# Sums of h made in place in the last product, and all logits and weight sums in the stage before it

## The chip, the cores and the metric

One core of a Trainium2 chip runs the whole program. Its engines work in parallel, each through its own queue in order: TensorE (PE) multiplies, VectorE (DVE) and ScalarE (ACT) do elementwise work, GpSimd (POOL) and SyncE (SP) issue transfers here. The metric is the device time of one execution in microseconds.

## The reference

With x of 2048 by 640, two DFT matrices per side and a gated feed-forward layer of width 1728, all float32:

```python
def _A_ref(x, dft_seq_re, dft_seq_im, dft_hid_re, dft_hid_im):
    a = jnp.einsum("bsd,ed->bse", x, dft_hid_re)
    b = jnp.einsum("bsd,ed->bse", x, dft_hid_im)
    return jnp.einsum("ts,bse->bte", dft_seq_re, a) - jnp.einsum("ts,bse->bte", dft_seq_im, b)

def _B_ref(x, w_gate, w_up, w_down):
    return (_gelu(x @ w_gate) * (x @ w_up)) @ w_down

g = _sigmoid((x * gate_w).sum(-1, keepdims=True))
return g * _A_ref(...) + (1 - g) * _B_ref(...)
```

## The kernel before, in words

**Arithmetic.** Every float32 operand is split into a high and a low part: ScalarE rounds the block (`high`, L80), VectorE subtracts that from the block (`low`, L83). A product of two blocks is three matmuls, high by high, high by low and low by high (L99 to L101). The large products use one level of a Strassen scheme: seven block products in place of eight, for which sums of blocks are needed on both sides. Such a scheme is run in two passes. A first pass takes the products that need the blocks themselves and one sum, a second pass those that need the other sums; partial results of the first are kept for the second. `X`, `Z`, `V`, `L`, `Q`, `R`, `Y` are the PSUM banks of the products, eight in all, so at a switch from one pass to the next a bank must be copied out (`copy`, L146, on ScalarE, or an addition on VectorE) before its successor starts.

**Stages.** (1) Up to about 325 us: gate and up product with the gelu. The result h is written to device memory in blocks `hA[tp][k]`: half `tp` of the rows, pair `k` of the width's tiles (six pairs), four parts of 128x512 each, b11, b12, b21, b22. (2) The *C stage*, to about 751 us: the sequence DFT times x. 64 steps `i`, each with one 1 MB piece of the matrix (`cra`, `crb`, loaded by `load_c` three steps ahead, split by `split_c` two steps ahead into `ch` and `cl`; in a second pass its sums are `csa` and `csb`). Steps 0 to 7 are a first pass, 8 to 15 a second, and so on in four groups. (3) The *last product* of the feed-forward layer, h by `w_down`, to about 927 us: 28 steps, for each half a first pass of seven and a second of seven (`load_k` three ahead, `split_k` two ahead, `step_k`). Its sums of h for the second pass are T1 = b12 - b11, T3 = b22 - b12, T2 = b22 - T1 and T4 = b21 - T2. (4) The hidden DFT, to the end, which adds onto the output.

**What stands between the steps of the C stage.** Four kinds of small work, each a few loads by SyncE, a few VectorE operations and stores by GpSimd:
- `sum_h` (twelve times, table `HT_AT`): loads the four parts of one `hA` block (`ht`), makes T1 to T4, stores them as `hT`, which the last product's second passes load.
- `sum_wd` (six times, `WD_AT`): sums of `w_down` for both passes (`dr`, `da`), stored as `wsd`.
- `sum_wu` (five times; three here, two in the last product): sums of the hidden DFT's weights (`ur`, `ua`), stored as `wsu`, with negated blocks `wneg`.
- `load_z` (sixteen times; ten here, six in the last product): a tile of x (`xz`), multiplied by `gate_w` and summed to logits in `z`. `gates` makes the sigmoid of the eight logits of one half and stores it and its complement.

`sum_h0_narrow` (twice, in the last product, `lg`) makes sums of the narrow remaining block of h, stored in `hL`.

**What sets the order.** ScalarE and VectorE keep the written order (`in_order`), SyncE's loads of the C stage too; TensorE's is made by a scheduler. Work that is loaded at step i is done at step i+1, after that step's split, so a load that is late holds everything written behind it on VectorE. In the last step of a first pass (7, 23, 39, 55) the split of the step two ahead is held until the first bank's products have been issued (`held`). All large tiles share 46 buffers of 4 KB per partition (`slot`), the 128x512 ones 15 buffers of 2 KB (`mtile`); a load or split waits until an earlier user of its buffer is done, for a stored tile until the store has landed.

Of the kernel before, what the change touches and what calls it, by code (L numbers as in the profile page):

```python
# [9 lines left out]
F32 = mybir.dt.float32  # L10
# [4 lines left out]
P = 128  # L15
# [10 lines left out]
GM_AT = [2,19]  # L26
EORD = [0, 2, 1, 3, 4]
PAIRED = 3
ZB_AT = [5,7,9,14,15,16]
XB_AT = [0, 1, 2, 3, 4, 5, 6, 7]  # L30
WU_AT, WU_DOWN = [18, 34, 49], [10, 17]
HL_AT = [1, 12]


@with_exitstack
def kernel(
# [33 lines left out]
    def slot(dt, shape, name):  # L70
        return pool.tile(shape, dt, tag="s4", name=name, bufs=46)
# [49 lines left out]
    gwb = pool.tile([P, D], F32, tag="gwb", name="gwb")  # L121


    hA, hT = ([[dram.tile([P, 4, T], F32, tag=f"h{n}{p}{k}", name=f"h{n}{p}{k}") for k in range(NK)] for p in range(2)] for n in "AT")
# [75 lines left out]
    def wsmall(dt, name):  # L200
        return pool.tile([P, 2, P], dt, tag="w", name=name, bufs=6)
# [405 lines left out]

    def sum_wd(k):

        r, a21 = slot(F32, [P, 8, P], f"dr{k}"), wsmall(F32, f"da{k}")  # L610
        nc.sync.dma_start(r, wd[k, :, :8])
        nc.sync.dma_start(a21, wd[k, :, 8:])
        return [do for _, do in sums_left(nc.gpsimd, r[:, 0:2], r[:, 2:4], r[:, 6:8], a21, wsd[k])]

    def sum_h(tp, k):


        b11, b12, b21, b22 = (mtile(F32, f"ht{tp}{k}{q}") for q in range(4))
        for q, v in enumerate((b11, b12, b21, b22)):
            nc.sync.dma_start(v, hA[tp][k][:, q])  # L620

        def do():
            tt(b11, b12, b11, op=ALU.subtract)  # L623
            keep(hT[tp][k], 0, b11)
            tt(b12, b22, b12, op=ALU.subtract)
            keep(hT[tp][k], 2, b12)
            tt(b22, b22, b11, op=ALU.subtract)
            keep(hT[tp][k], 1, b22)
            tt(b21, b21, b22, op=ALU.subtract)
            keep(hT[tp][k], 3, b21)  # L630

        return [do]

    def sum_h0(tp):

# [169 lines left out]
    def load_k(i):  # L805


        tp, b, k = kseq[i]
        n = f"{tp}{b}{k}"
        r = None  # L810
        if not (k == NK and b):
            r = slot(F32, [P, 8, P], f"kw{n}")
        if k == NK and b:
            src = hL[tp]
        elif k == NK:
            m = slot(F32, [P, 8, P], f"km{n}")
            d = slot(F32, [P, 8, P], f"kd{n}")
            nc.sync.dma_start(r[:, :5], wd0)
            for q in range(2):
                rows = slice(q * FR, (q + 1) * FR)  # L820
                nc.sync.dma_start(m[rows, :5], wdr)
                nc.sync.dma_start(d[rows, :4], wd0[:FR, :4])
            r, src = (r, m, d), h0[tp]
        elif b:
            nc.sync.dma_start(r[:, 0:2], wd[k, :, 6:8])
            nc.sync.dma_start(r[:, 2:8], wsd[k][:, 0:6])
            src = hT[tp][k]
        else:
            nc.sync.dma_start(r[:, 0:6], wd[k, :, 0:6])
            nc.sync.dma_start(r[:, 6:8], wsd[k][:, 6:8])  # L830
            src = hA[tp][k]
        raw = []
        for q in range(2):
            raw.append(pair(F32, f"kr{n}{q}"))
            nc.sync.dma_start(raw[q], src[:, 2 * q : 2 * q + 2])
        kraw[i] = r, raw

    def split_k(i):
        tp, b, k = kseq[i]
        n = f"{tp}{b}{k}"  # L840
        r, raw = kraw.pop(i)
        B = []

        def right():
            B = []
            for q in range(2):
                v = hl(f"kb{n}{q}")
                split(*v, raw[q])
                B += [at(v, 0), at(v, 1)]
            return B  # L850

        if k == NK and b:
            W = ktile.pop(("left", tp))
# [519 lines left out]
    for i, (j, ri, b, sp) in enumerate(cseq):  # L1373
# [2 lines left out]
        if i + AHEAD + 1 < len(cseq):  # L1376
            load_c(i + AHEAD + 1)
        ready, units = units, []
        if i in HT_AT:
            units += sum_h(*HT_AT[i])  # L1380
        if i in WD_AT:
            units += sum_wd(WD_AT[i])
        if i in ZC_AT:
            (_, first), (_, total) = load_z(1)
            first()
            units.append(total)
# [118 lines left out]
                after.append(tsums)  # L1505
    loads.close()

    zwork, narrow = [], []
    gates(0)
    for i in range(len(kseq)):  # L1510
        if i + 3 < len(kseq):
            load_k(i + 3)
# [16 lines left out]
        if i in GM_AT:  # L1529
            gm[GM_AT.index(i)] = gate_tile(gmd, GM_AT.index(i), f"gm{i}")  # L1530
        step_k(i)
        for do in narrow:
            do()
        narrow = sum_h0_narrow(HL_AT.index(i)) if i in HL_AT else []
        for p, at_i in enumerate(WU_DOWN, len(WU_AT)):
            if i == at_i:
                wus[p] = sum_wu(p)
            if at_i <= i < at_i + 3:
                next(wus[p], None)
        for _, do in zwork[:1]:  # L1540
            do()
        zwork = load_z(1) if i in ZB_AT else []
        for _, do in zwork[:1]:
            do()
        del zwork[:1]
        if i == ZB_AT[-1] + 1:
            gates(1)


    bk = {}  # L1550
# [225 lines left out]
```

## Time and profile before

| | |
|---|---|
| median of 3 runs | 1052.19 us (1050.69 to 1054.45) |
| profiled execution, its own time | 1054.85 us |
| its span, first to last instruction | 1053.1 us |
| TensorE busy | 1024.7 us (97%) |
| VectorE busy | 824.7 us (78%) |
| ScalarE busy | 486.3 us (46%) |
| GpSimd busy | 184.8 us (18%) |
| mean granted TensorE clock | 0.987 |
| moved by DMA | 280.95 MB, mean 267 GB/s |

A row of the timeline reads: start, duration, engine, line, operation, what is written and from what, count, and in brackets how long the engine stood idle before it and what ended that. Consecutive VectorE operations overlap a little, so the distance from one start to the next is what an operation costs the queue. Rows of waits give the total, how many, and the longest. Busy TensorE is not TensorE at its peak; the count of matmuls in a stretch tells more.

### The profile page before, as it was taken

What the parts mean: (1) busy time and instruction counts of PE and PEld (TensorE: products, weight loads), DVE (VectorE), ACT (ScalarE), POOL (GpSimd) and SP (SyncE); (2) the same over time, 40 slices, a digit from 0 to 9 for tenths busy, and PEclk for the clock granted to TensorE, in tenths of its full rate; (3) what the DMA queues carried; (4) which work ended last, traced back from release to release, by engine and by line L of the source; (5) the groups of instructions that cost most, each with busy time, mean ns of one, the idle gap of its engine ahead of it and who ended that gap; (6) DMA issues with size and microseconds to landing.
All of it is one profiled execution on the core that took longest, in us unless ns stands there. A gap on an engine that the chain in (4) does not pass through costs nothing.

```text
span 1053.1 us, 13358 instructions
## 1 busy us (share of the span) xinstructions
PE 1024.7 (97%) x4489; PEld 841.8 (80%) x4489; DVE 824.7 (78%) x1159; ACT 486.3 (46%) x624; POOL 184.8 (18%) x326
## 2 busy tenths in 40 slices
PE   9999999999999999996999899979999899999998
PEld 7888888888888878885888788868887688888887
DVE  8977755474758889856997798779979797996796
ACT  6644545444435744332342334333727736654350
POOL 0221111111201100221123302330210111011112
PEclk9999999999999999998999999989999999999999
DMA  8465455454668966898699889999899998987856
GB/s 308 147 211 196 126 178 162 152 170 137 185 204 292 259 195 215 285 368 281 235 324 378 335 314 312 380 412 384 293 336 374 399 385 325 352 324 219 265 158 98
DMA packets 101188, 280.95 MB, mean 267 GB/s; under 512 B 13504, under 2 KB 24640, under 8 KB 101120
## 3 DMA queue, kind: packets, MB, share of 16 engines
q1 hardware_dynamic: 73536, 194.15, 52.9%
q0 software_dynamic: 27296, 85.76, 25.2%
q8 instruction: 35, 0.57, 0.2%
q14 instruction: 33, 0.27, 0.1%
q10 hardware_dynamic: 288, 0.20, 0.1%
HBM read 205.06 MB, written 70.27 MB: 261 GB/s over the span
## 4 chain that ended last, share of the span: by engine, by line
issue 27%; PE 25%; DMA 7%; POOL 5%; DVE 2%; ACT 1%; SPq 0%; POOLq 0%; DVEq 0%; ACTq 0%
DMA xz<-in_xz 2%; POOL hT L415 1%; POOL uA L1359 1%; POOL uT L1359 1%; DMA ua<-in_wu 1%; DMA crb<-in_ct 1%; DMA ht<-hA 1%; DMA wneg<-ur 1%; PE yX L101 1%; PE yX L99 1%; PE yX L100 1%; PE kX L99 1%; DMA wsd<-dr 1%; PE kX L101 1%; PE kX L100 1%
## 5 line engine op out<-in xcount | busy, mean ns | idle before, releaser
L80 ACT ACTIVATE ch<-csa 128x1024 fp32r<-128x1024 f32 x32 | 34.0, 1062 | 121.0 <-DVE csa L786 107.8
L80 ACT ACTIVATE ch<-cra 128x1024 fp32r<-128x1024 f32 x32 | 33.9, 1058 | 70.1 <-DMA cra<-in_ct 17.1
L415 POOL DMA_DIRECT2D hA<-s x48 | 26.3, 547 | 179.2 <-DVE s L582 160.1
L83 DVE TENSOR_TENSOR cl<-crb,ch 128x1024 fp32r<-128x1024 f32 x32 | 39.1, 1221 | 22.4 <-DMA wsd<-dr 7.9
L415 POOL DMA_DIRECT2D hT<-ht x48 | 26.1, 544 | 157.5 <-DVE ht L623 149.4
L83 DVE TENSOR_TENSOR cl<-cra,ch 128x1024 fp32r<-128x1024 f32 x32 | 39.1, 1222 | 17.5 <-ACT ch L80 9.8
L100 PE MATMUL pL<-cl,xah 128*128 128x512 f32 x128 | 49.8, 389 | 0.0
L101 PE MATMUL pL<-ch,xal 128*128 128x512 f32 x128 | 49.8, 389 | 0.0
L99 PE MATMUL pL<-ch,xah 128*128 128x512 f32 x128 | 49.0, 389 | 0.0
L571 DVE TENSOR_TENSOR s<-s,pX 128x512 f32<-128x512 f32 x24 | 16.4, 685 | 38.5 <-PE pX L101 38.5
L80 ACT ACTIVATE ch<-crb 128x1024 fp32r<-128x1024 f32 x32 | 33.8, 1056 | 25.4 <-PE pL L101 8.9
L83 DVE TENSOR_TENSOR cl<-csb,ch 128x1024 fp32r<-128x1024 f32 x32 | 39.2, 1225 | 4.8 <-ACT ch L80 3.8
L83 DVE TENSOR_TENSOR cl<-csa,ch 128x1024 fp32r<-128x1024 f32 x32 | 39.0, 1220 | 4.6 <-ACT ch L80 3.5
L80 ACT ACTIVATE ch<-csb 128x1024 fp32r<-128x1024 f32 x32 | 33.9, 1060 | 12.0 <-DVE csb L789 6.1
L557 ACT ACTIVATE s<-pZ 128x512 f32<-128x512 f32 x24 | 14.2, 598 | 52.1 <-PE pZ L101 35.3
L99 PE MATMUL pX<-ch,xbh 128*128 128x512 f32 x64 | 25.4, 405 | 12.3 <-ACT ch L80 11.8
L576 ACT ACTIVATE s<-s 128x512 f32<-128x512 f32 x24 | 15.1, 634 | 46.6 <-DVE s L575 46.6
L80 ACT ACTIVATE kh<-kw 128x1024 fp32r<-128x1024 f32 x24 | 25.5, 1064 | 21.8 <-DMA kw<-wsd 21.8
L83 DVE TENSOR_TENSOR kl<-kw,kh 128x1024 fp32r<-128x1024 f32 x24 | 29.3, 1219 | 7.3 <-ACT kh L80 7.3
L146 ACT ACTIVATE s<-pX 128x512 f32<-128x512 f32 x41 | 23.7, 592 | 19.0 <-PE pX L101 18.7
L99 PE MATMUL pQ<-ch,xbh 128*128 128x512 f32 x64 | 26.6, 415 | 5.6 <-ACT s L146 5.6
L101 PEld LDWEIGHTS pL<-ch,xal 128*128 128x128 f32 x128 | 24.0, 188 | 5.0
(3658 smaller groups left out, 3478.5 us busy)
## 6 DMA issues: line engine op xcount, KB each, us to landing
cra<-in_ct SPq DMA_DIRECT2D x64, 512.0 KB, 6.3
crb<-in_ct SPq DMA_DIRECT2D x64, 512.0 KB, 6.4
hA<-s POOLq DMA_DIRECT2D x48, 256.0 KB, 2.9
ht<-hA SPq DMA_DIRECT2D x48, 256.0 KB, 7.8
hT<-ht POOLq DMA_DIRECT2D x48, 256.0 KB, 6.3
kr<-hA SPq DMA_DIRECT2D x24, 512.0 KB, 8.0
kr<-hT SPq DMA_DIRECT2D x24, 512.0 KB, 7.9
ux<-uA SPq DMA_DIRECT2D x24, 512.0 KB, 6.9
```

The costliest lines, as they stand in the source:

```text
L80: nc.scalar.activation(hi, raw, AF.Copy)
L83: nc.vector.tensor_tensor(lo, raw, hi.bitcast(F32), op=ALU.subtract)
L99: nc.tensor.matmul(ps, lh, rh, start=first, stop=False, skip_group_check=True)
L100: nc.tensor.matmul(ps, lh, rl, start=False, stop=False, skip_group_check=True)
L101: nc.tensor.matmul(ps, ll, rh, start=False, stop=last, skip_group_check=True)
L146: nc.scalar.activation(m, src, AF.Copy)
L415: nc.gpsimd.dma_start(to[:, i], src)
L557: nc.scalar.activation(s5, Z, AF.Copy)
L571: tt(s5, s5, X, op=ALU.add)
L576: nc.scalar.activation(s2, s2, AF.Gelu_apprx_tanh)
L1359: nc.gpsimd.dma_start(to[:, i], src)
```

## The change

`sum_h`, `HT_AT` and the blocks `hT` are gone. The second passes of the last product load the blocks `hA` themselves, and `split_k` makes the four sums in place on the loaded tiles before it splits them; since the sums then lie in another order than the products want them, the list that `right` returns is reordered. `sum_wd` loads into two `m` tiles instead of a large one and a small one. All five `sum_wu`, all sixteen logits and both `sum_h0_narrow` stand in the C stage, by tables of step numbers; both `gates` stand at the start of the last product. Two of the splits of x for second passes move from steps 6 and 7 to 9 and 11 (`XB_AT`).

```diff
-ZB_AT = [5,7,9,14,15,16]
-XB_AT = [0, 1, 2, 3, 4, 5, 6, 7]
-WU_AT, WU_DOWN = [18, 34, 49], [10, 17]
-HL_AT = [1, 12]
+XB_AT = [0, 1, 2, 3, 4, 5, 9, 11]
+WU_AT = [17, 19, 33, 35, 50]
+HL_AT = [21, 54]
+Z_AT = [18, 21, 26, 29, 30, 34, 37, 42, 45, 46, 49, 52, 55, 58, 61, 62]
...
     def sum_wd(k):
-        r, a21 = slot(F32, [P, 8, P], f"dr{k}"), wsmall(F32, f"da{k}")
-        nc.sync.dma_start(r, wd[k, :, :8])
-        nc.sync.dma_start(a21, wd[k, :, 8:])
-        return [do for _, do in sums_left(nc.gpsimd, r[:, 0:2], r[:, 2:4], r[:, 6:8], a21, wsd[k])]
-
-    def sum_h(tp, k):
...
+        r = [mtile(F32, f"dr{k}{q}").rearrange("p (b c) -> p b c", c=P) for q in range(2)]
+        nc.sync.dma_start(r[0], wd[k, :, 0:4])
+        nc.sync.dma_start(r[1], wd[k, :, 6:10])
+        return [do for _, do in sums_left(nc.gpsimd, r[0][:, 0:2], r[0][:, 2:4], r[1][:, 0:2], r[1][:, 2:4], wsd[k])]
...
-            src = hT[tp][k]
+            src = hA[tp][k]
...
         r, raw = kraw.pop(i)
+        sums = b and k < NK
+        if sums:
+            (b11, b12), (b21, b22) = ([v[:, q] for q in range(2)] for v in raw)
+            tt(b11, b12, b11, op=ALU.subtract)
+            tt(b12, b22, b12, op=ALU.subtract)
+            tt(b22, b22, b11, op=ALU.subtract)
+            tt(b21, b21, b22, op=ALU.subtract)
...
-            return B
+            return [B[q] for q in (0, 3, 1, 2)] if sums else B
...
-    HT_AT, WD_AT, ZC_AT = {}, {}, [16, 22, 26, 32, 38, 42, 48, 54, 58, 60]
-    for g in range(3):
-        for q, r in enumerate((2, 4, 8, 13)):
-            HT_AT[16 * g + 16 + r] = q % 2, 2 * g + q // 2
-        for q in range(2):
-            WD_AT[16 * g + 19 + 2 * q] = 2 * g + q
+    WD_AT = [20, 22, 36, 38, 51, 53]
...
-        if i in HT_AT:
-            units += sum_h(*HT_AT[i])
         if i in WD_AT:
-            units += sum_wd(WD_AT[i])
-        if i in ZC_AT:
+            units += sum_wd(WD_AT.index(i))
+        if i in HL_AT:
+            units += sum_h0_narrow(HL_AT.index(i))
+        if i in Z_AT:
...
-    zwork, narrow = [], []
-    gates(0)
+    for tp in range(2):
+        gates(tp)
...
-        for do in narrow:
-            do()
-        narrow = sum_h0_narrow(HL_AT.index(i)) if i in HL_AT else []
-        for p, at_i in enumerate(WU_DOWN, len(WU_AT)):
...
-        zwork = load_z(1) if i in ZB_AT else []
...
-        if i == ZB_AT[-1] + 1:
-            gates(1)
```

How it moves instructions, first on VectorE at the switch of the C stage into step 24: from the last operation of the split of step 24 (`cl24_1`) to the first of the split of step 25 (`csa25`). `dr`/`da` are a weight sum, `xz` a logit, `lg` a narrow sum of h. Before:

```order
L83 TENSOR_TENSOR cl24_1_4087<-csb24_4079,ch24_1_4086 128x1024
L597 TENSOR_TENSOR dr1_4020<-da1_4021,dr1_4020 128x256
L598 TENSOR_TENSOR da1_4021<-dr1_4020,da1_4021 128x256
L601 TENSOR_TENSOR dr1_4020<-dr1_4020 128x256
L730 ISA xz1_4074,z_63<-xz1_4074,gwb_64 128x640
L785 TENSOR_TENSOR csa25_4143<-cra25_4070 128x512
```

The change:

```order
L83 TENSOR_TENSOR cl24_1_4067<-csb24_4059,ch24_1_4066 128x1024
L645 TENSOR_TENSOR lg01_3991<-lg01_3991,lg00_3990 128x512
L646 TENSOR_TENSOR lg02_3992<-lg02_3992,lg03_3993 128x512
L648 TENSOR_TENSOR lg02_3992<-lg02_3992,lg01_3991 128x512
L711 ISA xz1_4000,z_63<-xz1_4000,gwb_64 128x640
L597 TENSOR_TENSOR dr11_4053<-dr11_4053 128x256
L598 TENSOR_TENSOR dr11_4053<-dr10_4052,dr11_4053 128x256
L601 TENSOR_TENSOR dr10_4052<-dr11_4053,dr10_4052 128x256
L766 TENSOR_TENSOR csa25_4127<-cra25_4048 128x512
```

Three operations of a narrow sum have come to a logit and a weight sum (of the weight sum one repeated row is left out, L602). At the switch into step 40 a logit and a weight sum stand there, at step 56 a weight sum and a narrow sum, at step 8 nothing.

The same place in SyncE's queue, from the loads of step 24 (`cra24`) to those of step 25. Before:

```order
L777 DMA cra24_4016<-in_ct 128x1024
L777 DMA crb24_4017<-in_ct 128x1024
L611 DMA dr1_4020<-in_wd 128x1024
L612 DMA da1_4021<-in_wd 128x256
L777 DMA cra25_4070<-in_ct 128x1024
```

The change:

```order
L758 DMA cra24_3986<-in_ct 128x1024
L758 DMA crb24_3987<-in_ct 128x1024
L640 DMA lg00_3990<-h00_77 64x512 x2
L640 DMA lg01_3991<-h00_77 64x512 x2
L642 DMA lg02_3992<-h00_77 128x512
L642 DMA lg03_3993<-h00_77 128x512
L707 DMA xz1_4000<-in_xz 128x640
L758 DMA cra25_4048<-in_ct 128x1024
```

Six loads of the narrow sum and one of a logit now stand ahead of the loads of step 25; the weight sum's loads have moved behind them.

Last, VectorE in a second pass of the last product: the split of its step for pair 2 of the first half (`kl` weights, `kb` h), with what stands next to it. Before:

```order
L83 TENSOR_TENSOR kl012_6820<-kw012_6753,kh012_6819 128x1024
L83 TENSOR_TENSOR kb0120l_6824<-kr0120_6756,kb0120h_6823 128x1024
L83 TENSOR_TENSOR kb0121l_6828<-kr0121_6758,kb0121h_6827 128x1024
L730 ISA xz11_6810,z_63<-xz11_6810,gwb_64 128x640
L83 TENSOR_TENSOR kl013_6862<-kw013_6812,kh013_6861 128x1024
```

The change:

```order
L826 TENSOR_TENSOR kr0120_6628<-kr0120_6628 128x512
L827 TENSOR_TENSOR kr0120_6628<-kr0121_6630,kr0120_6628 128x512
L828 TENSOR_TENSOR kr0121_6630<-kr0121_6630,kr0120_6628 128x512
L829 TENSOR_TENSOR kr0121_6630<-kr0121_6630 128x512
L83 TENSOR_TENSOR kl012_6698<-kw012_6625,kh012_6697 128x1024
L83 TENSOR_TENSOR kb0120l_6702<-kr0120_6628,kb0120h_6701 128x1024
L83 TENSOR_TENSOR kb0121l_6706<-kr0121_6630,kb0121h_6705 128x1024
L826 TENSOR_TENSOR kr0130_6689<-kr0130_6689 128x512
```

Four sums stand ahead of each of the ten such splits between the two evacuations (five in each half), and once more per half ahead of the first evacuation; the logits are gone.

More of the change, by code (lines that the diff above doesn't have):

```diff
@@ L121 @@
     gwb = pool.tile([P, D], F32, tag="gwb", name="gwb")
-    hA, hT = ([[dram.tile([P, 4, T], F32, tag=f"h{n}{p}{k}", name=f"h{n}{p}{k}") for k in range(NK)] for p in range(2)] for n in "AT")
+    hA = [[dram.tile([P, 4, T], F32, tag=f"hA{p}{k}", name=f"hA{p}{k}") for k in range(NK)] for p in range(2)]
     h0 = [dram.tile([P, 4, T], F32, tag=f"h0{p}", name=f"h0{p}") for p in range(2)]
@@ L608, in sum_wd @@
     def sum_wd(k):
-        r, a21 = slot(F32, [P, 8, P], f"dr{k}"), wsmall(F32, f"da{k}")
-        nc.sync.dma_start(r, wd[k, :, :8])
-        nc.sync.dma_start(a21, wd[k, :, 8:])
-        return [do for _, do in sums_left(nc.gpsimd, r[:, 0:2], r[:, 2:4], r[:, 6:8], a21, wsd[k])]
-    def sum_h(tp, k):
[L618 to L632, printed above, removed]
+        r = [mtile(F32, f"dr{k}{q}").rearrange("p (b c) -> p b c", c=P) for q in range(2)]
+        nc.sync.dma_start(r[0], wd[k, :, 0:4])
+        nc.sync.dma_start(r[1], wd[k, :, 6:10])
+        return [do for _, do in sums_left(nc.gpsimd, r[0][:, 0:2], r[0][:, 2:4], r[1][:, 0:2], r[1][:, 2:4], wsd[k])]
     def sum_h0(tp):
@@ L1531 @@
         step_k(i)
-        for do in narrow:
-            do()
-        narrow = sum_h0_narrow(HL_AT.index(i)) if i in HL_AT else []
-        for p, at_i in enumerate(WU_DOWN, len(WU_AT)):
[L1536 to L1541, printed above, removed]
-        zwork = load_z(1) if i in ZB_AT else []
-        for _, do in zwork[:1]:
-            do()
-        del zwork[:1]
-        if i == ZB_AT[-1] + 1:
-            gates(1)
     bk = {}
```

## The prediction

> **What bounds the kernel now.** I read the slices first, then the busy time by stretches, then TensorE's waits, then the neighbourhood of each wait on VectorE and in SyncE's queue.
>
> ```profile
> PEclk9999999999999999998999999989999999999999
> DMA  8465455454668966898699889999899998987856
> 400.00:480.00 80.00, 80.00 (x355) 66.24 (x353) 58.39 (x75) 28.38 (x29) 14.11 (x26) 1.00 0.83 297
> 380.00:400.00 20.00, 18.77 (x82) 14.88 (x82) 18.52 (x24) 11.07 (x14) 2.23 (x4) 1.00 0.61 211
> 480.00:520.00 40.00, 30.67 (x123) 24.27 (x122) 33.98 (x48) 13.43 (x16) 8.71 (x16) 0.87 0.73 248
> 580.00:620.00 40.00, 37.24 (x157) 30.30 (x156) 33.54 (x47) 14.07 (x18) 10.32 (x19) 0.96 0.91 333
> 700.00:720.00 20.00, 14.38 (x55) 11.39 (x54) 17.99 (x25) 8.31 (x10) 3.63 (x7) 0.83 1.03 403
> 820.00:860.00 40.00, 35.60 (x146) 28.91 (x145) 34.61 (x45) 24.81 (x29) 7.07 (x13) 0.91 1.03 385
> ```
>
> The stretch rows give, after its length, TensorE's busy time with its matmul count, then weight loads, VectorE, ScalarE, GpSimd, the granted clock, the DMA share and GB/s. At full rate 355 matmuls take 80 us, 0.225 us each. Counts below that rate are TensorE's lost time: in 380:400 6.75 matmuls are missing (88.75 less 82), 1.5 us; in 480:520 54.5, 12.3 us; in 580:620 20.5, 4.6 us; in 700:720 33.75, 7.6 us; in 820:860 31.5, 7.1 us. The first four, **26.0 us**, are the four switches of the C stage from a first to a second pass (steps 8, 24, 40, 56); the last, **7.1 us**, is the switch between the two halves of the last product. The rest runs at TensorE's rate: what this change can win is about 33 us.
>
> ```profile
> PE pX L99 <- ACT ch L80: 11.8, 3, 8.5
> PE pQ L99 <- ACT s L146: 5.6, 1, 5.6
> 601.28 0.50 PE L99 MATMUL pX<-ch,xbh 128*128 128x512 f32 x1 [2.76 <-ACT ch L80]
> 479.13 1.23 DVE L83 TENSOR_TENSOR cl<-crb,ch 128x1024 fp32r<-128x1024 f32 x1 [7.94 <-DMA wsd<-dr]
> SPq L777 <- DMA wsd<-dr: 14.3, 2, 7.8
> 701.79 0.83 DVE L730 CUSTOM_DVE_ANT_0 xz<-xz,gwb 128x640 f32<-128x640 f32 x1 [2.10 <-DMA xz<-in_xz]
> ```
>
> TensorE waits there for a split (`ch`) or for a bank copied behind a split, so VectorE or ScalarE is late. Why it is late differs. At step 24 VectorE stood 7.94 us for a buffer that the store of a weight sum (`dr`) still held. At step 40 SyncE's queue stood 14.3 us in two waits for such buffers and the next blocks were loaded late. At step 56 a logit tile (`xz`) came late while the DMA share was 1.03. At step 40, 2.76 us of idle cost 4.6 us in all: the clock stayed low for the other 1.8.
>
> **The change, part by part. Transfers.**
>
> ```profile
> ht<-hA SPq DMA_DIRECT2D x48, 256.0 KB, 7.8
> 480.27 0.69 DVE L623 TENSOR_TENSOR ht<-ht,ht 128x512 f32<-128x512 f32 x1
> 483.05 0.69 DVE L785 TENSOR_TENSOR csa<-cra 128x512 f32<-128x512 f32 x1
> ```
>
> 48 loads of 256 KB and as many stores go, 25 MB, with twelve blocks of four VectorE operations, 2.78 us each (480.27 to 483.05). The same four operations return in each of the twelve second-pass steps of the last product. Weight sums now stand in the 15 buffers of `m`, so the two waits on `wsd<-dr` above have no such buffer left to wait for; four T buffers per block are no longer asked of `m`, which pays for it.
>
> **The switches.** What came between the last two splits decides. The undisturbed model is step 8, where nothing but two x operations came between.
>
> ```profile
> 381.35 1.23 DVE L83 TENSOR_TENSOR cl<-csb,ch 128x1024 fp32r<-128x1024 f32 x1
> 384.52 0.69 DVE L785 TENSOR_TENSOR csa<-cra 128x512 f32<-128x512 f32 x1
> 386.85 0.39 PE L99 MATMUL pX<-ch,xbh 128*128 128x512 f32 x1
> 702.54 0.69 DVE L785 TENSOR_TENSOR csa<-cra 128x512 f32<-128x512 f32 x1
> 706.78 0.79 PE L99 MATMUL pQ<-ch,xbh 128*128 128x512 f32 x1 [5.62 <-ACT s L146]
> 487.93 0.42 DVE L597 TENSOR_TENSOR dr<-da,dr 128x256 f32<-128x256 f32 x1
> 489.65 0.82 DVE L730 CUSTOM_DVE_ANT_0 xz<-xz,gwb 128x640 f32<-128x640 f32 x1
> 490.39 0.69 DVE L785 TENSOR_TENSOR csa<-cra 128x512 f32<-128x512 f32 x1
> 775.64 0.68 DVE L664 TENSOR_TENSOR lg<-lg,lg 128x512 f32<-128x512 f32 x1
> 777.57 1.22 DVE L83 TENSOR_TENSOR kl<-kw,kh 128x1024 fp32r<-128x1024 f32 x1
> ```
>
> The split of the switch's own step ended at 382.58, 4.27 us before TensorE began that step (386.85); its first six matmuls cover 1.35 more. From the next split's first operation to TensorE going on takes 4.24 us (702.54 to 706.78). So TensorE waits for as long as VectorE works between the two splits, less 1.4 us. A weight sum takes 1.72 us there (487.93 to 489.65), a logit 0.74 (to 490.39), a narrow h sum 1.93 (775.64 to 777.57). After the change the order has, between those splits, at step 8 nothing (two x splits moved to steps 9 and 11): no wait; at step 24 a narrow sum, a logit and a weight sum, 4.39, a wait of 3.0; at step 40 a logit and a weight sum, 2.46, a wait of 1.1; at step 56 a weight sum and a narrow sum, 3.65, a wait of 2.25. To these I add the slow clock: 1.8 for the 3.0 (nearest row: 2.76 idle cost 1.8), half of that for 2.25, none for 1.1; and 2 us in all for loads that still land late, since of the traffic near the switches only part goes. That is 11.05 us of the 26.0 left, **15.0 saved**. Bounds: all 26.0 saved, if splits are made earlier with fewer buffers taken; only 5 saved, if each of the three late switches loses 2.5 to 4 us more to late loads (six loads of the narrow sum stand in SyncE's queue ahead of the next blocks at step 21, and right behind them at 54).
>
> The TensorE page of the Trainium skill (TensorE: Matmul & The Clock Gate, "What you observe" to "What's actually happening") says that the clock halves after an idle window of about 3.4 us. By that alone none of these idles would cost clock, nor would the one of 3.1 us below, and the sum would be 4.5 us lower. The row at 601.28 disagrees: 2.76 us of idle stood in a stretch with a mean clock of 0.96. I keep the row.
>
> **The last product.** TensorE's second-pass step is 24 matmuls, 5.4 us.
>
> ```profile
> 785.21 0.43 DVE L856 TENSOR_TENSOR km<-km 128x256 f32<-128x256 f32 x1 [4.15 <-DMA km<-in_wdr]
> 800.46 1.28 DVE L973 TENSOR_TENSOR ks<-ks,kV 128x512 f32<-128x512 f32 x2
> 802.40 1.22 DVE L83 TENSOR_TENSOR kl<-kw,kh 128x1024 fp32r<-128x1024 f32 x1
> 805.81 1.28 DVE L926 TENSOR_TENSOR ks<-ks,gm 128x512 f32<-128x512 f32 x2
> 808.22 1.22 DVE L83 TENSOR_TENSOR kl<-kw,kh 128x1024 fp32r<-128x1024 f32 x1
> 840.24 1.29 DVE L985 TENSOR_TENSOR ks<-ks,ks 128x512 f32<-128x512 f32 x2
> 842.18 0.80 PE L99 MATMUL kZ<-kb1001h,kh 128*128 128x512 f32 x1 [4.40 <-DVE ksa L985]
> 888.30 1.38 DVE L973 TENSOR_TENSOR ks<-ks,kV 128x512 f32<-128x512 f32 x2 [4.99 <-ACT ks L146]
> 911.34 1.22 DVE L83 TENSOR_TENSOR uw00l<-uw00r,uw00h 128x1024 fp32r<-128x1024 f32 x1
> 918.16 1.22 DVE L83 TENSOR_TENSOR ub11l<-ux,ub11h 128x1024 fp32r<-128x1024 f32 x1
> 927.15 0.39 PE L99 MATMUL yX<-ub00h,uw00h 128*128 128x512 f32 x1
> ```
>
> A split is 3.41 us (802.40 to 805.81); with the sums ahead of it, 6.19, which is 0.8 more than TensorE's step: VectorE now sets the pace there. Between evacuating the first pass (L973) and the second (L985) it has five such splits, 30.95, and four gated outputs, 2.41 (805.81 to 808.22).
>
> First half: before, L973 stood at 800.46. The six loads and the three operations of the narrow sum and the T block ahead of it are gone, and with them most of the 4.15 wait at 785.21; its own split brings 2.78. I take 799 (bounds: 797.6, when TensorE ends that pass, and 803.2). Then 1.2, 30.95, 2.41 and two plain splits, 6.82, reach L985 at 840.4; before it was 840.24, with three logits, a weight sum and load waits in that stretch, all gone now. `kZ`, two operations later (1.94, as 840.24 to 842.18), starts when it did. But TensorE's wait of 4.40 falls apart: 2.7 of it are now spent waiting for splits, so the slow clock, 7.1 less 4.4, **2.7, is saved**. Bounds: 4 saved, 4.3 lost.
>
> Second half: L973 waits for TensorE as before and ends at 889.68. To it come 30.95, 2.41 and the seven plain splits of the next product, 7.96 (911.34 to 918.16 and 1.14): L985 at 931.0. TensorE's last step starts at 923.0 (889.68 and 33.36), ends at 928.4; six matmuls of `yX` reach 929.8; the next product's second banks are free at 932.95. Before, they were taken six matmuls after 927.15, at 928.5. So **4.45 are lost**, with 3.1 of idle and 1.8 of clock, **6.25**. Bounds: 3 (no clock, one step's lateness absorbed) and 9.
>
> What I cost at nothing: both gate steps at the start (VectorE and ScalarE under 0.25 us each, beside the first steps' products); six logits, two narrow sums, two weight sums elsewhere in the C stage, 0.74, 1.93 and 1.72 us of VectorE, hidden while first-pass steps leave it two thirds idle (a first-pass split is 2.4 us against 6.76 of TensorE); if that cover went, they would cost their own length at the next switch, at most 3 us.
>
> **Sum.** 15.0 and 2.7 saved, 6.25 lost: 11.4 less than the profiled execution's 1054.85 (span 1053.1), 1043.4. The median of the runs shown is 2.66 lower, 1052.19: **1041**. By the Trainium skill's rule alone it would be an estimated 1036.
>
> **Rivals.**
> *The switches vanish* (24 in 100). For it: the two waits on `wsd<-dr` are removed at their cause, and 25 MB less lets loads land early. Against it: 2.5 to 4.4 us of sums still stand between the splits. 26.0 and 2.7 saved, 6.25 lost: 1030.
> *The switches stay late* (17 in 100): the DMA share is still near 1 ahead of them, since the narrow sums and a second weight sum took the T blocks' place, and a load that is late holds VectorE in order. Only 8 saved there; 4.5 in all: 1048.
> *VectorE's queue in the second passes costs more than the C stage gives* (11 in 100, slower). In its favour: it has no slack there at all, and its first operation on a block now waits for the load itself. If L973 of the first half comes at 803.2 and one wait like that at 785.21 (4.15) falls into each pass, the halves lose 4.3 and 4.15, then 4.45, 4.15 and 2.7 of clock: 19.8 against 15.0, 1057. It decides once the second passes cost over 18.2. Against it: in the second half the loads were ahead of VectorE from 889 to 919.
> *The forecast* has 48 in 100, and its own range is 1034 to 1048. **Range** for all: 1027 to 1052, from just below the first rival to half way into the last.
>
> A measurement of this kernel tells about 0.3%, 3.2 us, from no change. Faster by more: 47 of the forecast's 48, the 24, and 11 of the 17: 0.82. Within it: 1, 5, and 1 of the slower case: 0.07. Slower, 1 of the 17 and 10 of the last: 0.11.
>
> **What would show it.** No `ht` and no `wsd<-dr` among the waits; the counts of the four switch stretches up from 82, 123, 157 and 55; step 8 without a gap, step 24 still with the longest. In the last product, VectorE without idle between L973 and L985, TensorE waiting for `kb` splits by under 1 us a step, and a new wait of `yZ` for L985 of about 3 us, which was not there. Wrong would be: a wait of the same length at steps 40 and 56 (then late loads, not buffers, made it), `yZ` without a wait (VectorE had slack I did not see), or new waits for `m` buffers in SyncE's queue.

## The result and the profile after

The changed kernel takes 1036.15 us, the median of four runs (1035.35 to 1037.92). The kernel before, run beside it, takes 1053.32. The ratio is 0.984, with a 95% interval from 0.982 to 0.987: 17 us faster, of which the prediction had named 11.

Slices of the changed kernel, for the two rows shown of before:

```profile
PEclk9999999999999999999999999999999999989999
DMA  8556364554567976699769877999899879967856
```

Stretches of the changed kernel (columns as in the prediction). Its times are earlier than before's by whatever was saved up to that point, so step 56 now lies in 680:720, the switch between the halves in 800:840, the end of the last product in 880:920:

```profile
380.00:400.00 20.00, 20.00 (x90) 16.57 (x89) 17.70 (x23) 10.78 (x14) 2.23 (x4) 1.00 0.65 217
480.00:520.00 40.00, 38.99 (x172) 31.89 (x171) 38.61 (x54) 16.95 (x19) 4.90 (x9) 1.00 0.76 253
520.00:540.00 20.00, 18.37 (x81) 14.71 (x81) 14.67 (x21) 8.60 (x11) 2.78 (x6) 1.00 0.62 226
580.00:620.00 40.00, 40.00 (x177) 32.82 (x176) 37.18 (x51) 17.62 (x20) 4.34 (x8) 1.00 0.75 254
680.00:720.00 40.00, 40.00 (x178) 33.15 (x177) 39.52 (x52) 21.21 (x24) 2.72 (x5) 1.00 0.99 353
800.00:840.00 40.00, 37.01 (x158) 30.20 (x157) 39.86 (x48) 23.45 (x27) 3.25 (x6) 0.96 0.82 266
880.00:920.00 40.00, 36.14 (x147) 29.01 (x146) 39.76 (x48) 26.24 (x28) 3.26 (x6) 0.91 0.82 285
```

A full stretch of 40 us holds 177.5 matmuls. The four switches, which had lost 26.0 us, now show 90 in 20 us (step 8; 88.75 is the full rate), 172 (step 24), 177 (step 40) and 178 (step 56). Step 56 runs at TensorE's rate although the DMA share there is still 0.99: traffic alone was not what made it late. A place that lost nothing before now loses 2 us: 520:540, where a second pass gives way to a first (step 32). VectorE is busy for 39.86 and 39.76 of 40 us in the two last stretches, the two ends of the last product's halves.

TensorE's waits in the changed kernel (engine, line, released by: total, times, longest):

```profile
PE yZ L99 <- DVE ksa L973: 3.2, 1, 3.2
PE kZ L99 <- DVE ksa L973: 3.0, 1, 3.0
PE pX L99 <- ACT s L146: 1.6, 1, 1.6
PE pX L99 <- ACT ch L80: 1.0, 1, 1.0
```

Two waits for VectorE's second evacuation (L973, before L985) are the bulk: the known one of `kZ` between the halves, and a new one of `yZ` in the next product. The other two are steps 32 and 24.

The first matmul of the last product shows what the C stage gave back; before, and then the changed kernel:

```profile
751.08 0.39 PE L99 MATMUL kX<-kb0000h,kh 128*128 128x512 f32 x1
```

```profile
728.95 0.39 PE L99 MATMUL kX<-kb0000h,kh 128*128 128x512 f32 x1
```

Read so, from the first matmul of one stage to the first of the next (the last stage to the start of its last matmul), the stages of the profiled executions are these. Most of these executions lie within 1.6 us of the median beside them; that of `no_t` is 3.1 us above it and that of `lead` 3.2 us below. The three parts of the change are: T sums in place, weight sums in `m`, and all logits and sums moved into the C stage.

| kernel | parts | median us | C stage | last product | hidden DFT |
|---|---|---|---|---|---|
| before | none | 1053.3 | 425.8 | 176.1 | 122.4 |
| after | all | 1036.15 | 403.3 | 172.8 | 128.7 |
| `wd_m` | weight sums in m | 1041.4 | 415.9 | 173.1 | 122.4 |
| `t_only` | T in place | 1052.3 | 409.5 | 184.4 | 127.7 |
| `t_wd` | T in place, weight sums in m | 1044.1 | 400.7 | 183.5 | 129.0 |
| `no_t` | weight sums in m, moved | 1059.9 | 439.0 | 171.3 | 122.4 |
| `wd_slot` | T in place, moved | 1052.9 | 420.3 | 172.9 | 128.8 |
| `sums_out` | all, sums left out | 1023.85 | 403.1 | 167.3 | 122.4 |
| `lead` | all, and one step of lead | 1030.07 | 403.2 | 170.3 | 122.4 |
| `table` | all, steps moved | 1031.7 | 399.1 | 171.6 | 128.8 |
| `q_first` | all, Q evacuated first | 1032.2 | 403.3 | 171.6 | 126.2 |
| `all_three` | the last three together | 1023.6 | 399.9 | 171.1 | 122.4 |
| `all_four` | and the evacuation earlier | 1020.55 | 399.5 | 168.1 | 122.4 |

By stage the change gave 22.5 us in the C stage and 3.3 in the last product, and lost 6.3 in the hidden DFT, whose first six matmuls stand ahead of the wait of `yZ`. That is 19.5 together; the span fell by 19.2.

### The profile page after: what moved, and what is told of

It is laid out like the page before. It is cut to its first block, busy times and chain, and to the rows that moved or that the text cites. A ratio compares the mean times of both kernels' runs of the same rounds, so it can differ in the third digit from the quotient of the medians.

```text
span 1033.9 us, 13156 instructions
## 1 busy us (share of the span) xinstructions
PE 1019.6 (99%) x4489; PEld 838.6 (81%) x4489; DVE 824.7 (80%) x1159; ACT 487.4 (47%) x624; POOL 158.8 (15%) x278
## 4 chain that ended last, share of the span: by engine, by line
PE 95%; DVE 2%; issue 1%; DMA 1%; ACT 1%; SPq 0%; DVEq 0%; ACTq 0%
PE pX L99 7%; PE pX L101 6%; PE pX L100 6%; PE pZ L101 5%; PE pZ L100 5%; PE pZ L99 5%; PE pL L99 3%; PE pL L100 3%; PE pL L101 3%; PE pV L100 2%; PE pV L101 2%; PE pV L99 2%; PE pQ L99 1%; PE pQ L101 1%; PE pQ L100 1%; PE pR L100 1%
## 5 line engine op out<-in xcount | busy, mean ns | idle before, releaser
L915 POOL DMA_DIRECT2D out<-ks x12 | 6.5, 544 | 162.5 <-DVE ks L914 161.9
L1347 POOL DMA_DIRECT2D uA<-c x8 | 4.3, 542 | 168.3 <-DVE c L1463 168.1
L99 PEld LDWEIGHTS pL<-ch,xah 128*128 128x128 f32 x128 | 24.0, 188 | 5.9 <-DVE sa L1457 0.9
L100 PEld LDWEIGHTS pL<-cl,xah 128*128 128x128 f32 x128 | 24.0, 188 | 4.9
```

Of the source, the lines that this page charges most:

```text
L99: nc.tensor.matmul(ps, lh, rh, start=first, stop=False, skip_group_check=True)
L100: nc.tensor.matmul(ps, lh, rl, start=False, stop=False, skip_group_check=True)
L915: nc.gpsimd.dma_start(acc4[:, t] if tp and e == 4 else out[2 * tp + t, e], src)
```

## The experiments: which part of the change did it

My theory after the result had two halves that could be told apart. Either the T blocks (their `m` buffers and their 25 MB) had made the switches late, or the slots held by the stores of the weight sums had. Five kernels leave out parts of the change.

**`t_only`: before, with the T sums in place alone.**

```
-            src = hT[tp][k]
+            src = hA[tp][k]
+            tt(b11, b12, b11, op=ALU.subtract)     # and the three others, in split_k
-            HT_AT[16 * g + 16 + r] = q % 2, 2 * g + q // 2
```

> The kernel before, with one part of the change alone: the T sums of h are made in place in the second passes of the last product, and no T block is loaded, summed or stored in the C stage. Weight sums, logits and narrow sums stay where they were. Theory 1 (the T blocks' buffers and transfers made the switches late): the four switches keep about 5 of their 26.0 us; the last product, whose VectorE now has the T sums beside the logits and the narrow sums, loses about 17; about 1042. Theory 2 (the weight sums' slots, held by their stores, made them late): the waits on the store of the weight sum stay, the switches keep about 22 us, and with the same 17 in the last product about 1059.

Measured: 1052.33 us, ratio 0.999 (0.997 to 1.001), no change beyond the noise. It lies between the two expectations: the C stage fell by 16.3 us, steps 24 and 40 still lost 4.6 and 4.2 (ahead of them ScalarE stood 10.2 and 10.9 us for a buffer that the store of a weight sum held), step 56 lost nothing, and the last product with the stage behind it rose by 13.6, since VectorE had the T sums beside the logits.

**`no_t`: the changed kernel with the T sums back in the C stage.**

```
-            src = hA[tp][k]                        # second pass, and no sums in split_k
+            src = hT[tp][k]
+        if i in HT_AT:
+            units += sum_h(*HT_AT[i])
```

> The changed kernel with the T sums put back into the C stage (12 blocks of four loads, four sums and four stores at the old steps); the last product loads the ready sums again. Logits, weight sums and narrow sums stay in the C stage. Theory 1: the switches lose at least 15 us again, the last product loses none of its 11.7: 1035 or more. Theory 2: the switches keep what the smaller weight-sum buffers gave, about 8 us are lost there and none in the last product: about 1028.

Measured: 1059.91 us, ratio 1.0075 (1.005 to 1.010): slower than the kernel before. In TensorE's waits of this run:

```profile
PE pX L99 <- ACT ch L80: 23.1, 3, 9.2
```

Three switches wait for splits again, up to 9.2 us. Sums that the C stage holds easily without the T blocks do not fit beside them. Theory 1 is right that the T blocks matter.

**`wd_slot`: the changed kernel with the weight sums back in slots.**

```
-        r = [mtile(F32, f"dr{k}{q}").rearrange("p (b c) -> p b c", c=P) for q in range(2)]
+        r, a21 = slot(F32, [P, 8, P], f"dr{k}"), wsmall(F32, f"da{k}")
```

> The changed kernel with the weight sums back in a slot and a small weight tile, as before the change; steps, loads and everything else as changed. Theory 2 (a slot held by the store of the weight sum made steps 24 and 40 late): waits on that store come back on SyncE or VectorE and the switches lose 5 to 15 us: 1041 to 1051. Theory 1 (with the T blocks gone the slots suffice anyway): within 3 us of the changed kernel, 1036.

Measured: 1052.86 us, ratio 0.999 (0.997 to 1.001). One buffer choice undone takes back all of the change's gain, 16.7 us. Its waits, ScalarE's and TensorE's:

```profile
ACT ch L80 <- DMA wsd<-dr: 6.0, 1, 6.0
483.40 1.06 ACT L80 ACTIVATE ch<-csb 128x1024 fp32r<-128x1024 f32 x1 [5.97 <-DMA wsd<-dr]
PE pX L99 <- ACT ch L80: 11.4, 2, 6.7
480.00:520.00 40.00, 32.89 (x133) 26.19 (x132) 32.37 (x46) 14.48 (x17) 4.88 (x9) 0.87 0.60 212
```

ScalarE stands 6.0 us because the next tile of a split is the slot that a weight sum's store still holds. VectorE's part of that split and the whole of the next stand behind it, TensorE waits 6.7 for the next, and 44.5 matmuls are missing in the stretch. Its DMA share of 0.60 is a mean and says little of the wait itself: while ScalarE stood (477.4 to 483.4) the share was about 0.9, and the stores, issued from 474.1 us on, had to land beside that traffic.

**`wd_m`: before, with the weight sums in `m` alone** (the same line, the other way round).

> The kernel before, with the weight sums of the C stage in two tiles of m instead of a slot and a small tile; the T blocks, logits and everything else stay. If a slot held by a store is a cause that stands alone, the two waits on the store of the weight sum go and steps 24 and 40 lose 8 us less or more: 1044 or below. If m, from which the T blocks take four tiles each, is short then, the waits only change their buffer: within 3 us of 1052.5, or slower.

Measured: 1041.40 us, ratio 0.989 (0.986 to 0.992). The first expectation holds: this one line gives 12 of the change's 17 us. (It also leaves out two blocks that a weight sum does not use, 0.8 MB in all of the kernel's 281; the waits on the store that it removes speak for the buffer.) TensorE still waits at three switches:

```profile
PE pQ L99 <- ACT s L146: 10.5, 3, 4.8
SPq L659 <- DMA hT<-ht: 12.0, 1, 12.0
```

The first row is the bank copy that stands behind a late split, at steps 24, 40 and 56. The second shows `m` under pressure: SyncE stands 12.0 us ahead of a narrow sum's load until a T block's store has landed.

**`t_wd`: before, with both, the logits left in the last product.**

> The kernel before, with the T sums in place in the last product and the weight sums in m, but logits, narrow sums and two weight sums left in the last product, so without the second half of the change. If each part has its price by itself: the C stage loses about 4.5 us as in the changed kernel, the last product about 22 as in the run with the T sums alone: 1046. If the logits and sums in the last product cost nothing beside the T sums: about 1036, as the whole change.

Measured: 1044.09 us, ratio 0.992 (0.990 to 0.994), 2 below the additive expectation. With the T blocks gone and the weight sums in `m`, steps 24, 40 and 56 lose nothing:

```profile
480.00:520.00 40.00, 40.00 (x178) 33.16 (x177) 38.10 (x51) 18.90 (x21) 4.33 (x8) 1.00 0.69 232
PE kZ L99 <- DVE ksa L992: 6.6, 1, 6.6
PE yZ L99 <- DVE ksa L992: 3.2, 1, 3.2
PE kX L99 <- ACT ks L146: 2.0, 1, 2.0
PE kX L100 <- DVE kb0121l L83: 1.8, 1, 1.8
```

Now the last product pays: 6.6 us between the halves, 3.2 at the end, and 3.8 in two more waits. Moving the logits and sums out of it (the step from this run to the changed kernel) gives 10.9 us there and costs 2.6 in the C stage: about 4.2 lost at steps 24, 32, 40 and 48, less the 1.8 that this run still loses at step 8. The table shows that the parts do not add: T in place is worth nothing alone; the move costs 18.5 us where the T blocks stay (`no_t` against `wd_m`) and gives 8 where they are gone (`t_wd` against the changed kernel). Either the T blocks or the slots of the weight sums were enough to keep some of the switches late, and not the same ones. Step 56 loses nothing wherever the T blocks are gone (`t_only`, `wd_slot`, `t_wd`), and 7.2 and 11.0 us where they stay (`wd_m`, `no_t`); the slots alone hold up steps 24 and 40. Whether the T blocks act by their `m` buffers, their transfers or their VectorE time, no run separates.

## The experiments: what the last product lost

**`sums_out`: no T sums in the last product.**

```
-            tt(b11, b12, b11, op=ALU.subtract)
-            tt(b12, b22, b12, op=ALU.subtract)
-            tt(b22, b22, b11, op=ALU.subtract)
-            tt(b21, b21, b22, op=ALU.subtract)
```

> The changed kernel without the four T sums of each second-pass block of the last product (the blocks are split as they are loaded, so four of its seven products are of other operands); all loads, splits and matmuls stay. Pace theory (VectorE's 6.2 us a step against TensorE's 5.4 is what makes the two evacuations late): the 4.6 us lost between the halves and the 7.1 at the end fall to under 1 in all: about 1025. Rival (the order of the queue, with the splits of the next steps ahead of the evacuation, makes it late whatever the sums cost): at least 5 of the 11.7 stay: 1030 or more.

Measured: 1023.85 us, 12.3 below the changed kernel. The last product takes 167.3 instead of 172.8 and the hidden DFT 122.4 instead of 128.7: all of the loss in both stages is the 2.78 us of sums in each block, none of it the order of the queue alone.

**`lead`: one more step of lead.** VectorE is not busy all the time. In the changed kernel it stands still ahead of the second half's first evacuation:

```profile
862.08 1.38 DVE L961 TENSOR_TENSOR ks<-ks,kV 128x512 f32<-128x512 f32 x2 [7.35 <-ACT ks L146]
904.67 1.28 DVE L973 TENSOR_TENSOR ks<-ks,ks 128x512 f32<-128x512 f32 x2
906.61 0.79 PE L99 MATMUL yZ<-ub01h,uw00h 128*128 128x512 f32 x1 [3.24 <-DVE ksa L973]
```

It idles 7.35 us at 862 and is 3.24 us late at 904. Splits made one step earlier would fill the first and shorten the second.

```
-        if i + 3 < len(kseq):
-            load_k(i + 3)
+        for q in [i + 3, i + 4] if i == LEAD else [i + 3 + (i > LEAD)]:    # LEAD = 3
+            if q < len(kseq):
+                load_k(q)
```

and `split_k` likewise, from i + 2 to i + 3.

> The changed kernel with one more step of lead in the last product from its fourth step on: blocks are loaded four steps ahead instead of three and split three steps ahead instead of two. Nothing else moves. If the loss is a backlog of VectorE that its idle time in the first passes (7.35 us ahead of the first-pass evacuation at 862) can take up, each half has 6.2 us of work less behind that evacuation and the 11.7 us fall to about 1: about 1025. If loads or buffers hold VectorE instead, or the extra blocks take slots that others wait for, less than 4 us are won: 1032 or more.

Measured: 1030.07 us (the profiled execution 1026.89, the three others 1030.0 to 1030.8), ratio 0.979 (0.977 to 0.982), between the two expectations. The profiled execution has a mean granted clock of 1.00, the others 0.997 or 0.998; over their length that is worth an estimated 2 to 3 us, which goes with most of the difference; where in these three executions the clock fell, no trace shows. The end of the second half loses nothing any more; the first half still does:

```profile
880.00:920.00 40.00, 40.00 (x178) 33.15 (x177) 39.90 (x46) 24.29 (x27) 3.25 (x6) 1.00 0.89 328
PE kZ L100 <- DVE ksa L974: 2.5, 1, 2.5
```

There the further split (three steps ahead) stands ahead of the evacuation in VectorE's queue and takes back what the lead gave.

**`q_first`: the order of two pairs of sums in the second evacuation.**

```
-        for to, v, w in ((c12, c12, s2), (a, s2, Q), (c12, c12, R), (s2, a, R), (a, a, Y)):
+        for to, v, w in ((a, s2, Q), (c12, c12, s2), (c12, c12, R), (s2, a, R), (a, a, Y)):
```

> The changed kernel with the two first pairs of sums of the second evacuation exchanged: the bank pair Q, which the next step's second product waits for, is read before the output sum that needs no bank. If the second product waits for VectorE to read Q, each half waits 1.2 us less: 1033.7, and down to 1030 if the shorter idle times are followed by less of the slow clock. If another bank or ScalarE's copy comes next, nothing changes: 1036.

Measured: 1032.21 us, 3.9 below the changed kernel, within the expectation.

```profile
PE yZ L99 <- DVE ksa L973: 2.0, 1, 2.0
PE kZ L99 <- DVE ksa L973: 1.8, 1, 1.8
PE kV L99 <- DVE ks L973: 1.0, 1, 1.0
PE yV L99 <- DVE ks L973: 1.0, 1, 1.0
880.00:920.00 40.00, 36.34 (x158) 29.08 (x157) 39.79 (x47) 27.34 (x29) 3.25 (x6) 1.00 0.79 279
```

Each wait is 1.2 us shorter, and a wait of 1.0 for the next bank pair comes behind it, so the idle time hardly falls. What falls is the slow clock: in the same stretch the granted clock is 1.00 instead of 0.91, with 158 matmuls instead of 147.

## The experiments: the switches, and a faster kernel

**`table`: other steps in the C stage.**

```
-Z_AT = [18, 21, 26, 29, 30, 34, 37, 42, 45, 46, 49, 52, 55, 58, 61, 62]
+Z_AT = [16, 19, 25, 26, 27, 34, 37, 42, 43, 44, 49, 52, 55, 58, 61, 62]
-    WD_AT = [20, 22, 36, 38, 51, 53]
+    WD_AT = [18, 20, 36, 38, 51, 53]
```

> The changed kernel with other steps for three things in the C stage: the weight sums of steps 20 and 22 at 18 and 20; the logits of steps 18, 21, 26, 29, 30, 45, 46 at 16, 19, 25, 26, 27, 43, 44. Between the last two splits ahead of step 24 then stands a narrow sum alone, 1.93 us, and no logit takes a slot within two steps of the switches back to first passes at 32 and 48. By the prediction's rule (TensorE waits for the work between the two splits less a lead, the lead now 3.2 us as measured at step 24) the gap of 1.40 goes; if the logits' slots are what delayed step 32 (2.02) and 48 (0.68), those go: 3.7 less, 1032.4. If late loads or VectorE's pace in the second passes made them, they stay: within 1 us of 1036.

Measured: 1031.68 us, 4.5 below the changed kernel, 0.7 under the expectation.

```profile
480.00:520.00 40.00, 40.00 (x178) 33.12 (x177) 35.90 (x49) 16.24 (x19) 2.71 (x5) 1.00 0.67 235
520.00:540.00 20.00, 20.00 (x90) 16.57 (x89) 18.34 (x24) 10.95 (x13) 5.23 (x10) 1.00 0.81 270
```

Steps 24 and 32 both run at TensorE's rate. The gap of step 24 was the work between its two splits; the gap of step 32 came with the logits just ahead of it. That it was their slots is likely (in the changed kernel ScalarE stood 3.29 us, to 530.21, for a buffer that TensorE was still reading, right ahead of the late copy) but not separated from their VectorE time. The edit touches the C stage alone, which gave 4.2 us in the profiled execution; its last product is 1.2 shorter too, by the clock, as the last section shows.

**`all_three`: lead, table and Q first.**

> The changed kernel with the further step of lead, the moved table and bank pair Q first together. If the three gains stand apart: the run with the lead (1030.1) less 3.7 and less 1.2 for the first half, whose wait was left there: about 1025. If the earlier splits and the moved logits want the same slots: 1028 or more.

Measured: 1023.58 us, ratio 0.972 (0.968 to 0.976), 1.4 below the expectation. What was left, 3.3 us, stood between the halves. **`all_four`** takes it up:

```
-            if q < len(kseq):
+            if q < len(kseq) and i != 13:
                 split_k(q)
...
         step_k(i)
+        if i == 13:
+            split_k(16)
```

> The run with all three edits, and one more: in the last step of the last product's first half the evacuation stands ahead of VectorE's next split instead of behind it. In the run without this TensorE still loses 3.3 us there, in two gaps of 2.03 and 1.43. If VectorE's queue is the cause, about 2 of it go: 1021.5. If the copy of the bank by ScalarE and the two first sums are the chain that is left, less than 1: 1023 or more.

Measured: 1020.55 us (1019.92 to 1021.10), ratio 0.969 (0.968 to 0.971) to the kernel before, 15.6 us below the changed kernel. Its page and its longest waits of TensorE:

```profile
span 1019.3 us, 13151 instructions
PEclk9999999999999999999999999999999999999999
PE kX L100 <- ACT ks L147: 0.5, 1, 0.5
PE pQ L100 <- ACT s L147: 0.4, 1, 0.4
```

The gain over the kernel before, 32.8 us, is what the prediction put up as the most that could be won (26.0 and 7.1). TensorE's rate is the bound now; by the waits that are left, further edits to the order of VectorE can win an estimated 1 us.

## Why the prediction was right, and where it was not

**What bounds it: right.** The losses were the four switches and the switch between the halves, and nothing else: the fastest kernel gains their sum.

**The cause of the late switches: right for the weight sums, short on the T blocks.** Buffers held by the store of a weight sum were named as the cause at steps 24 and 40; `wd_m`, `wd_slot` and `t_only` show it. One such wait is left in the changed kernel, 2.1 us of ScalarE at 580.5, now for an `m` tile, and step 40 loses 0.3 us at most. The T blocks were named as what paid for the cure and as traffic. In the C stage they weigh more than the slots: taken out alone they gave 16.3 us there (`t_only`) against 9.9 (`wd_m`), and put back they cost 35.7 (`no_t`) against 17.0 (`wd_slot`). That `wd_m` is nevertheless the faster of the two single edits lies in the last product, where the T sums cost `t_only` its gain.

**The switches' sum, 15.0: mis-sized; 22.5 measured.** The failed step is the lead in "TensorE waits for as long as VectorE works between the two splits, less 1.4 us". The form held, the 1.4 did not. It came from step 8, where the split of the switch's own step was ready 4.27 us before TensorE began it. In the changed kernel, at step 24:

```profile
478.40 1.23 DVE L83 TENSOR_TENSOR cl<-csb,ch 128x1024 fp32r<-128x1024 f32 x1 [0.20 <-PE pL L100]
479.54 0.69 DVE L645 TENSOR_TENSOR lg<-lg,lg 128x512 f32<-128x512 f32 x1
483.93 0.69 DVE L766 TENSOR_TENSOR csa<-cra 128x512 f32<-128x512 f32 x1
485.15 0.39 PE L99 MATMUL pX<-ch,xbh 128*128 128x512 f32 x1
487.69 0.74 PE L99 MATMUL pX<-ch,xbh 128*128 128x512 f32 x2 [1.01 <-ACT ch L80]
672.41 1.23 DVE L83 TENSOR_TENSOR cl<-csb,ch 128x1024 fp32r<-128x1024 f32 x1
680.41 0.68 DVE L766 TENSOR_TENSOR csa<-cra 128x512 f32<-128x512 f32 x1
685.43 0.39 PE L99 MATMUL pX<-ch,xbh 128*128 128x512 f32 x1
```

The split ends at 479.54 and TensorE begins at 485.15: 5.61 us of lead, and 1.35 of first matmuls. From the next split's first operation (483.93) to TensorE going on (487.69) are 3.76. So 3.2 us of work between the splits cost nothing; there were 4.39 (479.54 to 483.93), which leaves 1.2 by this sum and 1.0 in the row, where I had 3.0 and then 1.8 of slow clock that did not come. At step 40 the lead was 6.8 us (579.67 to 586.43). At step 56 the split ended at 673.55 (672.41 and the 1.14 to the next operation), 11.9 us before 685.43, and the 6.9 us to the next split, load waits included, cost nothing. Step 8 was not the model for the others that I took it for. One of its splits stood behind TensorE for a slot (1.07 us at 380.10 before; at step 24 that wait is 0.20), and in the changed kernel, where no x split stands between its last two splits any more, it still does:

```profile
380.48 1.22 DVE L83 TENSOR_TENSOR cl<-csa,ch 128x1024 fp32r<-128x1024 f32 x1 [1.08 <-PE pL L100]
```

Its lead there is still 4.3 us, so the short lead belongs to the place; why, is open. At steps 24 and 40 the runs show buffers to set the lead: in `wd_slot`, with the same work on VectorE, both splits ended 0.6 us after TensorE had begun the step (485.63 against 485.00 at step 24), while step 56 kept 12.2 us of lead. My upper bound said just that ("if splits are made earlier with fewer buffers taken") and I priced the middle by the row with the least lead. The 2 us for late loads did not come at the four switches; 2.7 came at steps 32 and 48 instead, which I had not looked at, since no gap stood there before.

**Step 8: right.** With the two x splits moved it has no gap; `t_wd` and `wd_m`, which leave them, keep its 1.8.

**First half of the last product, 2.7 saved: right in sum, by another path.** The stage as a whole gave 3.3. I expected TensorE to wait for splits on the way, and the slow clock to go. There is no wait for a split of `kb` among TensorE's; VectorE began its second evacuation 3.1 us earlier than forecast (815.2; 840.4 less the 22.1 by which the stage now starts earlier is 818.3), because the first evacuation came that much earlier (773.8, where the forecast's 799 less 22.1 is 776.9), ahead of the lower bound that I gave it: it waits for ScalarE's copy of a bank, not for the end of the pass.

```profile
773.76 1.38 DVE L961 TENSOR_TENSOR ks<-ks,kV 128x512 f32<-128x512 f32 x2 [1.65 <-ACT ks L146]
815.21 1.29 DVE L973 TENSOR_TENSOR ks<-ks,ks 128x512 f32<-128x512 f32 x2
```

So `kZ` waits 3.0 instead of 4.4 and a slow clock follows, 1.5 us instead of 2.7; two small gaps at 752 and 800, which I had left out, went too, 1.4 together, and one of 0.6 came at the stage's end. That the sum agreed was luck.

**Second half, 6.25 lost: right.** 6.3 by the stage times, with the new wait of `yZ` (3.2) for the line I named and 2.7 of slow clock behind it; of the forecast's 6.25 the lateness was 4.45 and the clock 1.8, so it has the clock too small and the lateness too large.

**What I costed at nothing** was not nothing: the logits and sums elsewhere in the C stage opened the gaps at steps 32 and 48, 2.7 us, inside the 3 that I had set if their cover went. I had looked for that loss at the switches to second passes; it came at those back to first passes.

**Rivals.** "The switches vanish" came nearest in its C stage, 26.0 against the 22.5 measured and the forecast's 15.0; in all its 1030 is 6 us off, the forecast's 1041 5 us. "Stay late" fell. The slower rival was closer than its 11 in 100 looks: in `t_only` and `t_wd` the last product and the stage behind it cost 13.6 and 14.0 us against those of before, and in `t_only` that ate the gain. The move of the logits is what kept it away.

**The rule of the Trainium skill** that I weighed (TensorE: Matmul & The Clock Gate, "What you observe" to "What's actually happening") gave 1036, the measured time, but not for its reason: by it no idle here costs clock, while 4.2 us were lost to it in the changed kernel. The agreement is the C stage's missing 7.5 us.

## What to carry to other kernels

A tile whose buffer is released by a store belongs in another pool than the tiles on the critical path: here one line of that kind was worth 12 us alone and 17 beside the rest. Before moving work into a stage, find what sets the producer's lead there (here, at two of the four switches, free buffers), and read it at each switch rather than at one. When an engine in order is late at one place and idle a few steps ahead of it, one more step of lead and the right place of the evacuation cost nothing: with two small reorderings they gave another 15.6 us.

## What the runs showed that I had not expected

Whether an idle time is followed by a slow clock is not set by its length alone. The same wait of `kZ` stands in the changed kernel and in `table`; these are the matmul behind it and the stretch, first of the changed kernel:

```profile
817.15 0.80 PE L99 MATMUL kZ<-kb1001h,kh 128*128 128x512 f32 x1 [2.99 <-DVE ksa L973]
800.00:820.00 20.00, 17.01 (x70) 13.65 (x69) 19.90 (x25) 16.89 (x20) 0.00 (x0) 0.92 0.87 267
```

and of `table`:

```profile
812.69 0.50 PE L99 MATMUL kZ<-kb1001h,kh 128*128 128x512 f32 x1 [3.02 <-DVE ksa L973]
800.00:820.00 20.00, 16.98 (x75) 13.53 (x73) 20.00 (x23) 17.70 (x21) 0.00 (x0) 1.00 0.81 263
```

2.99 us of idle cost 1.5 more in the one, 3.02 cost nothing in the other. The records of the granted clock in the traces show what does decide. Each slow stretch runs at half the clock and lasts 3.41, 6.83 or 10.24 us (the end of a span may cut it short), and in every run the starts lie whole multiples of 3.413 us apart: the clock is set on a fixed grid. Cutting the span from 335 us on by that grid, in all 13 traces, gives one rule without an exception: a window in which TensorE stood idle (between matmuls, by their modelled ends) for 1.79 us or more is followed by a slow one, 27 of 27; one at full clock with 1.76 us or less is not, in some 2,500, of which 27 had over 1 us of idle. In the changed kernel the wait of `kZ` puts 2.49 us into one window (813.24 to 816.65). In `table` a border at 811.24 parts it into 1.57 and 1.45.

Short waits in one window add up: in `t_wd` waits of 0.28 and 1.81 us make 2.09, and 1.7 us of slow clock follow. The profiled execution of `q_first` kept its clock by the same rule: its waits of 2.0 and 1.0 leave no window with more than 1.71. An idle time of 2.08 us that fell into one window was enough in `no_t`, with 1.7 us lost; one of 2.51 was not in the profiled execution of `lead`, where a border leaves 1.75 at most. From 3.2 us on a slow clock always came, and the loss behind one idle time was never above 3 us, however long it had lasted. The page of the Trainium skill named above says that the window runs freely, so that its phase decides; that agrees with the grid. Its 3.4 us as the least idle time does not: about half a window sufficed.

For a forecast, an idle time that stands alone costs no clock below 1.8 us, and from there to an estimated 3.5 us (twice 1.76, the most that a border can part) it has a price between nothing and 3 us, by luck of the phase. Cutting it below 1.8, or parting it by some matmuls as `q_first` did, can be worth more than the idle time itself.
